# Moving weight preparation and accumulator copies by a tick in a fused Fourier / two-layer MLP kernel

## The chip, the cores and the metric

The kernel runs on one core of a Trainium2 chip. The metric is the device time of one launch in microseconds. Three runs of the kernel before gave 958.94, 959.30 and 959.51 us (median 959.3 us).

## What is computed

The input `x` has the shape (2, 3008, 256). The real part of its two-dimensional Fourier transform over the last two axes goes, as 6016 rows of 256 numbers, through two feed-forward layers of hidden width 2048, in float32:

```python
X = np.fft.fft(x, axis=1); X = np.fft.fft(X, axis=2); x = X.real.reshape(6016, 256)
h = x @ w_in
g = np.where(h > 0.0, h, np.exp(np.minimum(h, 0.0)) - 1.0)
x = g @ w_out
h = x @ w2_in
g = np.maximum(h, 0.0) + alpha * np.minimum(h, 0.0)
out = g @ w2_out
```

## The kernel before

**Numbers and blocks.** Products run on TensorE in a shortened float type. To keep float32 accuracy an operand is split into a rounded part, hi (written by ScalarE), and the rest, lo (written by GpSimd or VectorE), and a product is made in three passes: hi by hi, lo of the weight by hi, hi of the weight by lo (`PASSES`, line 465). The 6016 rows are cut into six blocks, each of two tiles (t = 0 and 1) of up to 512 columns. The last part of the transform, over the 256 columns, is folded into the first layer's `w_in`: `w_fold(c)` (lines 376 to 406) multiplies chunk c, a quarter of the hidden width, by a constant matrix with full float32 products (line 381) and splits the result.

**Ticks.** Layer one is 96 ticks, written out by the host loop in lines 900 and 901. One tick handles 128 hidden units f of one block. `SEGS` (line 42) sets the order: block 0 with f 0 to 7 in ticks 0 to 7, block 1 with f 0 to 7 in ticks 8 to 15, block 0 with f 8 to 15 in ticks 16 to 23, block 1 with the same in ticks 24 to 31, and then four blocks of 16 ticks. Tick t does, in this order on each engine's queue:

- the "pre" hooks of the tick;
- `gemm1(t)` on TensorE, six products (line 477), then on VectorE the correction `pt` (line 610) and the two halves `ht` (line 614), which read the product's two PSUM banks;
- on ScalarE hi of tick t-2 (line 589), then the "mid" hooks;
- if tick t-3 was the last of a segment (t = 10, 18, 26, 34, 50, 66, 82), `gemm2(t-3)` now, and the copy of the accumulators' t = 0 half by VectorE (`evac`, line 626);
- on ScalarE the relu (line 630) and the exponential (line 636 through tick 41; from tick 42 line 641, which writes two PSUM banks);
- on GpSimd lo of tick t-2 (line 595), on VectorE the combination of tick t-1 (line 582 or 579);
- in those seven ticks, the copy of the accumulators' t = 1 half (line 647). Where a segment starts at f = 0 (t = 10, 18, 50, 66, 82) ScalarE makes these copies, two of them (line 511);
- the "end" hooks, and in all other ticks `gemm2(t-3)`, twelve products (line 493).

For a segment's first f (but block 0's f = 0) and for its last, `gemm2` takes the three passes of each of the four accumulators one after the other; in the others the four lo passes come last. In both orders the second product of a `gemm2` reads lo of the weight.

**Weights.** A chunk of `w_out` is unpacked by ScalarE (`conv_y`, line 338) and by three VectorE steps (lines 356, 358 and 360), and then split in two halves (`w_split`, lines 412 to 423): each half has one ScalarE copy for hi (line 435) and one GpSimd subtraction for lo (line 436). `CONV1` (lines 53 to 58) lists, for a chunk, the tick of `conv_y` (a "mid" hook), the ticks of the three steps and the ticks of the two halves of the split (all of them "end" hooks, lines 776 to 783). Chunk 2 is read from f = 8 on, first by the `gemm2` in tick 19, and chunk 3 from f = 12 on, first by the `gemm2` in tick 23. `FOLD` (line 64) places `w_fold` of chunks 2 and 3, `STAGE_A1` (line 60) the first transform step of the second batch: `stage_a(1, c, i)` (lines 181 to 193) is two full float32 products (line 187) and two ScalarE copies (line 189). `KEEP` (lines 71 to 78) loads and unpacks second-layer chunks during layer one (load in the first tick given, `conv_y` and first step in the second tick, steps two and three in every second tick after). `PREP_0` (line 81) prepares the second layer's first operands; `b11` is one ScalarE copy ("mid") and one GpSimd subtraction ("end").

PSUM has eight banks: four accumulators, two "mm" and two "ee". Before tick 42 `gemm1`, `stage_a` and `w_fold` take the mm pair and the ee pair in turn; from tick 42 `gemm1` has the mm pair alone and the exponential the ee pair.

The second layer (pairs, lines 705 to 766) starts after tick 95, at about 463 us.

Of the kernel before, what the change touches and what calls it, by code (L numbers as in the profile page):

```python
# [43 lines left out]
E_PSUM = 42  # L44
# [8 lines left out]
CONV1 = [  # L53
    (('i', 1, 2), 8, (8, 9, 11), ()),
    (('i', 1, 3), 11, (12, 13, 14), ()),
    (('o', 1, 2), 14, (14, 15, 16), (17, 18)),
    (('o', 1, 3), 18, (18, 20, 21), (21, 22)),
]

STAGE_A1 = [  # L60
    (0, (7, 'pre'), (8, 'pre')), (1, (9, 'pre'), (11, 'pre')), (2, (12, 'pre'), (14, 'pre')), (3, (16, 'pre'), (17, 'pre')),
]
LOAD_X = {3: 9}
FOLD = {2: (13, 'pre', 0), 3: (15, 'mid', 0)}
LOAD_V = {(0, 2): 12, (1, 0): 24, (1, 1): 24, (1, 2): 24}
STAGE_B = {(0, 1): 5, (0, 2): 22, (1, 2): 32, (1, 0): 36, (1, 1): 40}
LOAD_ZB = {1: 6, 2: 29, 3: 45, 4: 61, 5: 77}
# [2 lines left out]

KEEP = [
    (("i", 2, 0), 31, 34, 81),
    (("o", 2, 0), 36, 39, 84),
    (("i", 2, 1), 45, 48, 88),
    (("o", 2, 1), 52, 55, 92),
    (("i", 2, 2), 59, 61, 95),
# [1 line left out]
]  # L78
FINAL_1 = [(84, "i", 0, 0), (86, "i", 0, 1), (88, "o", 0, 0), (90, "o", 0, 1), (92, "i", 1, 0), (94, "i", 1, 1)]
DIRECT = {("o", 2, 2): 95, ("o", 2, 3): 0}  # L80
PREP_0 = [("x", 62), ("t3", 64, 65), ("t1", 67, 68), ("b11", None, 69), ("t2", 74, 75), ("b21", None, 76), ("t4", 78, 82),
          ("b22", None, 83)]
FIRST = [
# [21 lines left out]
def tile_fft_moe_elu_moe_prelu(  # L105
# [361 lines left out]
    def gemm1(bl, f, two):  # L467
        n = BLOCKS[bl][2]
        c, o = divmod(f, 4)
        fs = slice(o * 128, (o + 1) * 128)  # L470
        w = wi[1, c]
        ps2 = []
        for t in range(2):
            p = mmtile(two)
            ops = [(w[:, a, t, fs], zt[bl][:, b, t, 0:n]) for a, b in PASSES]
            for i, (lhsT, rhs) in enumerate(ops):
                mm(out=p[:, 0:n], lhsT=lhsT, rhs=rhs, start=(i == 0), stop=(i == len(ops) - 1))  # L477
            ps2.append(p[:, 0:n])
        return ps2
# [16 lines left out]
    def evac(L, bl, f, first, last, ts, ds=(0, 1)):  # L496
        n = BLOCKS[bl][2]
        ac = accs[L, bl]
        if L == 1 and bl not in xs:
            xs[bl] = big.tile([128, 2, 2, 512], F32, tag="big", name="xs")  # L500
        for t in ts:
            for d in ds:
                if L == 1:
                    o = xs[bl][:, d, t, 0:n]
                else:
                    ot = wk.tile([128, 512], F32, tag="s", name="ot", bufs=4)
                    o = ot[:, 0:n]
                if first > 0:
                    tt(out=o, in0=ac[d][t][:, 0:n], in1=xs[bl][:, d, t, 0:n], op=ALU.add)
                elif t == 1:  # L510
                    act(out=o, in_=ac[d][t][:, 0:n], func=ACTF.Copy)  # L511
                else:
                    nc.vector.tensor_copy(out=o, in_=ac[d][t][:, 0:n])
                if L == 2:
                    for g, a, c0, m in pieces(bl):
                        nc.sync.dma_start(out=out[d * 128:(d + 1) * 128, c0 + t * BLK_N[g]:c0 + t * BLK_N[g] + m],
                                          in_=o[:, a:a + m])
            if L == 1 and last == NFT - 1 and 1 in ds:
                nc.sync.dma_start(out=xd[bl][:, :, t, 0:n], in_=xs[bl][:, :, t, 0:n])

    def pieces(bl):

        b, g, n = BLOCKS[bl]
        at_ = lambda b_, g_: 2 * (b_ * HALF + sum(BLK_N[:g_]))
        if bl != LONG:
            return [(g, 0, at_(b, g), n)]
        b0, g0, n0 = BLOCKS[SHORT]
        return [(g, 0, at_(b, g), n - MOVED), (g0, n - MOVED, at_(b0, g0) + n0, MOVED)]
# [39 lines left out]
    ticks = [(1, bl, f, f0, f1 - 1) for bl, f0, f1 in SEGS for f in range(f0, f1)]  # L568
    NT = len(ticks)
    LAG = 3  # L570

    def parts(t):
        return (slice(0, 1), slice(1, 2)) if t == 0 else (slice(0, 2),)

    def combine(t, some=None):
        s = st[t]
        if "x" in s:
            for i in range(2):
                stt(out=s["e"][:, i, :], in0=s["x"][i], scalar=-1.0, in1=s["h"][:, i, :], op0=ALU.add, op1=ALU.max)  # L579
        else:  # L580
            for i in some or parts(t):
                stt(out=s["e"][:, i], in0=s["e"][:, i], scalar=-1.0, in1=s["h"][:, i], op0=ALU.add, op1=ALU.max)  # L582

    def split_hi(t):
        s = st[t]
        s["hi"] = wk.tile([128, 2, 512], F32R, tag="hi", name="hi")
        s["lo"] = wk.tile([128, 2, 512], F32R, tag="lo", name="lo")
        for i in parts(t):
            act(out=s["hi"][:, i, 0:s["n"]], in_=s["e"][:, i], func=ACTF.Copy)  # L589

    def split_lo(t):
        s = st[t]
        n = s["n"]
        for i in range(2):
            nc.gpsimd.tensor_tensor(  # L595
                out=s["lo"][:, i, 0:n], in0=s["e"][:, i, :], in1=s["hi"][:, i, 0:n].bitcast(F32), op=ALU.subtract)

    def tick(t, pre, mid, end):
        cur = ticks[t] if t < NT else None
        for fn in pre:  # L600
            fn()
        if cur:
            L, bl, f = cur[:3]
            n = BLOCKS[bl][2]
            p = gemm1(bl, f, t >= E_PSUM)
            ht = wk.tile([128, 2, 512], F32, tag="h", name="ht")
            et = wk.tile([128, 2, 512], F32, tag="e", name="et", bufs=3)
            st[t] = dict(n=n, f=f, h=ht[:, :, 0:n], e=et[:, :, 0:n])
            pt = wk.tile([128, 512], F32, tag="s", name="pt", bufs=4)
            stt(out=pt[:, 0:n], in0=zb[bl][:, 0:n], scalar=an_sb[:, f:f + 1], in1=p[0], op0=ALU.mult, op1=ALU.add)  # L610
            for i, op in enumerate((ALU.add, ALU.subtract)):
                if t == 1:
                    combine(0, parts(0)[i:i + 1])
                tt(out=ht[:, i, 0:n], in0=pt[:, 0:n], in1=p[1], op=op)  # L614
        if t == 1:
            split_hi(0)
            split_lo(0)
        if t - 2 in st and t > 3:
            split_hi(t - 2)
        for fn in mid:  # L620
            fn()
        over = t < NT and t - LAG in st and ticks[t - LAG][2] == ticks[t - LAG][4]
        if over:
            s = st.pop(t - LAG)
            gemm2(*ticks[t - LAG], s["hi"], s["lo"])
            evac(*ticks[t - LAG], (0,))
        if cur:
            s = st[t]
            for i in parts(t):
                act(out=s["e"][:, i], in_=s["h"][:, i], func=ACTF.Relu, scale=-1.0)  # L630
                if t == 2:
                    combine(1)
                    split_hi(1)
                    split_lo(1)
                if t < E_PSUM or t == NT - 1:
                    act(out=s["e"][:, i], in_=s["e"][:, i], func=ACTF.Exp, scale=-1.0)
            if E_PSUM <= t < NT - 1:
                s["x"] = []
                for i in range(2):
                    s["x"].append(ps.tile([128, 512], F32, tag="ee", name="eet", bufs=2)[:, 0:s["n"]])  # L640
                    act(out=s["x"][i], in_=s["e"][:, i, :], func=ACTF.Exp, scale=-1.0)  # L641
        if t - 2 in st and t > 3:
            split_lo(t - 2)
        if t - 1 in st and t > 2:
            combine(t - 1)
        if over:
            evac(*ticks[t - LAG], (1,))
        for fn in end:
            fn()
        u = {2: 0, 3: None}.get(t, t - LAG)  # L650
        if u in st and t < NT:
            last_1(u)

    def last_1(u):
        s = st.pop(u)
        gemm2(*ticks[u], s["hi"], s["lo"])
# [113 lines left out]
    def at(t, fn, *a, where="pre"):  # L770
        hooks[where].setdefault(t, []).append(lambda: fn(*a))

    def at2(p, fn, *a, where="pre"):
        hooks[where].setdefault(1000 + p, []).append(lambda: fn(*a))
# [16 lines left out]
    with tc.manual_schedule():  # L791
# [45 lines left out]
        at(9, load, ("o", 1, 2))  # L837
        for c, (t, where, n) in FOLD.items():
            at(t, w_fold, c, where=where)
# [48 lines left out]
        for bl in range(2, NBLK):  # L888
            for i, (pre, mid) in enumerate(AHEAD):
                for where, todo in (("pre", pre), ("mid", mid)):  # L890
                    for what, *args in todo:
                        at2(bl * NFT // 2 - len(AHEAD) + i, does[what], bl, *args, where=where)
        for name, t, *cs in PREP_0:
            if name == "x":
# [5 lines left out]
        for t in range(NT):  # L900
            tick(t, *(hooks[w].get(t, []) for w in ("pre", "mid", "end")))
# [88 lines left out]
```

## Time and profile before

| | us |
|---|---|
| median of three runs | 959.3 |
| the profiled execution, its own time | 959.1 |
| its span from first to last instruction | 957.3 |
| TensorE busy | 945.2 |
| VectorE busy | 716.1 |
| ScalarE busy | 654.3 |
| GpSimd busy | 627.4 |

Times in the rows are microseconds from the start of the span. PE is TensorE's products, PEld its weight loads, DVE VectorE, ACT ScalarE, POOL GpSimd. A row of the timeline merges like instructions that follow each other: start, time from the first one's start to the last one's end, engine, line, operation, what is written and read, shapes and types, count, and in brackets the idle time of the engine just before and what ended it. The end of a product is modelled; successive products overlap, so their starts are what counts.

### The profile page before, as it was taken

The page shows a single profiled execution, that of the slowest core. Times are in us where ns is not written, and L with a number is a line of the kernel's source. Part 1 is how long each engine was busy: PE and PEld are TensorE (multiplying, and loading weights), DVE is VectorE, ACT ScalarE, POOL GpSimd, SP SyncE. Part 2 cuts the span into 40 slices and gives each one's busy share as a digit, 9 for nine tenths or more (in the row PEclk, how much of TensorE's full clock was granted, in tenths as well). Part 3 has the DMA queues.
Part 4 walks back from the last instruction along what each step waited for, and adds up shares of the span by engine and source line. Part 5 has one row for each costly group of instructions (what it writes and reads, how often), then busy time and mean ns, then how long its engine had stood idle before and what let it go on. Part 6 is the DMA issues. An engine that isn't in the chain of part 4 may idle for free.

```text
span 957.3 us, 12202 instructions
## 1 busy us (share of the span) xinstructions
PE 945.2 (99%) x4206; PEld 768.5 (80%) x4206; DVE 716.1 (75%) x1015; ACT 654.3 (68%) x915; POOL 627.4 (66%) x495
## 2 busy tenths in 40 slices
PE   9999999999999999999999999999999999999998
PEld 3677678799888877888888888889988888888886
DVE  2899899989999998887787675565666567566564
ACT  5778777767788887888765665656566566565553
POOL 1366578755968779987878855647565664664543
PEclk9999999999999999999999999999999999999999
DMA  8966222311322210130230110020020011001001
GB/s 326 321 187 161 58 78 88 100 49 41 100 84 98 90 45 34 45 110 22 69 130 1 39 45 0 7 83 1 1 73 10 0 45 45 1 1 45 0 1 45
DMA packets 27189, 64.10 MB, mean 67 GB/s; under 512 B 3124, under 2 KB 11572, under 8 KB 25080
## 3 DMA queue, kind: packets, MB, share of 16 engines
q1 hardware_dynamic: 25696, 62.09, 19.6%
q10 hardware_dynamic: 1176, 1.07, 0.3%
q8 instruction: 33, 0.54, 0.2%
q0 software_dynamic: 256, 0.17, 0.1%
q14 instruction: 28, 0.23, 0.1%
HBM read 41.53 MB, written 21.79 MB: 66 GB/s over the span
## 4 chain that ended last, share of the span: by engine, by line
PE 83%; DVE 10%; issue 2%; ACT 2%; POOL 1%; ACTq 0%; DVEq 0%; POOLq 0%
PE acc L493 45%; PE eet L672 13%; PE mmt L672 10%; PE mmt L477 7%; DVE ht L614 2%; DVE et L582 2%; PE eet L477 2%; DVE pt L610 2%; PE mmt L187 1%; DVE w L358 1%; POOL lo L595 1%; DVE et L579 1%; DVE w L360 1%; PE eet L381 1%; ACT et L630 1%
## 5 line engine op out<-in xcount | busy, mean ns | idle before, releaser
L493 PE MATMUL acc<-hi,wo 128*128 128x512 f32 (+1 forms) x1536 | 429.4, 386 | 2.8 <-ACT hi L589 1.5
L698 POOL TENSOR_TENSOR lo<-et,hi 128x512 fp32r<-128x512 f32 (+1 forms) x190 | 237.6, 1281 | 180.8 <-ACT hi L692 180.8
L595 POOL TENSOR_TENSOR lo<-et,hi 128x512 fp32r<-128x512 f32 (+1 forms) x192 | 276.3, 1461 | 94.4 <-ACT hi L589 48.9
L493 PEld LDWEIGHTS acc<-hi,wo 128*128 128x128 f32 x1536 | 287.9, 188 | 59.5 <-ACT xs L511 2.2
L493 PE MATMUL acc<-lo,wo 128*128 128x512 f32 (+1 forms) x768 | 258.4, 387 | 1.0 <-POOL lo L595 1.0
L692 ACT ACTIVATE hi<-et 128x1024 fp32r<-128x1024 f32 (+1 forms) x96 | 100.3, 1045 | 132.2 <-PE acc L493 69.9
L493 PEld LDWEIGHTS acc<-lo,wo 128*128 128x128 f32 x768 | 143.3, 188 | 30.9 <-POOL lo L595 3.9
L630 ACT ACTIVATE et<-ht 128x1024 f32<-128x1024 f32 (+2 forms) x97 | 100.3, 1034 | 64.0 <-DVE ht L614 62.2
L724 DVE TENSOR_TENSOR v<-mmt,p 128x512 f32<-128x512 f32 (+1 forms) x48 | 32.7, 680 | 143.0 <-ACT p L719 142.8
L477 PE MATMUL mmt<-zt,wi 128*128 128x512 f32 (+1 forms) x438 | 113.1, 391 | 0.8 <-DVE ht L614 0.4
L589 ACT ACTIVATE hi<-et 128x1024 fp32r<-128x1024 f32 (+2 forms) x97 | 99.4, 1024 | 5.5 <-DVE et L582 4.1
L614 DVE TENSOR_TENSOR ht<-pt,mmt 128x512 f32<-128x512 f32 (+1 forms) x148 | 93.8, 675 | 8.0 <-DVE pt L610 0.5
L477 PEld LDWEIGHTS mmt<-zt,wi 128*128 128x128 f32 x438 | 81.8, 188 | 19.9 <-issue 1.5
L749 ACT ACTIVATE et<-mmt 128x512 f32<-128x512 f32 (+1 forms) x96 | 55.8, 589 | 28.9 <-PE mmt L672 14.6
L582 DVE SCALAR_TENSOR_TENSOR et<-et,ht 128x1024 f32<-128x1024 f32 (+2 forms) x44 | 67.1, 1525 | 1.4 <-POOL lo L595 1.1
L610 DVE SCALAR_TENSOR_TENSOR pt<-zb,an_sb,mmt 128x512 f32<-128x512 f32 (+1 forms) x72 | 52.7, 731 | 20.0 <-PE mmt L477 19.9
L579 DVE SCALAR_TENSOR_TENSOR et<-eet,ht 128x512 f32<-128x512 f32 (+1 forms) x106 | 67.1, 675 | 0.0
L752 DVE SCALAR_TENSOR_TENSOR et<-et,oma_sb,eet 128x512 f32<-128x512 f32 (+1 forms) x96 | 66.1, 730 | 0.0
L752 DVE SCALAR_TENSOR_TENSOR et<-et,oma_sb,mmt 128x512 f32<-128x512 f32 (+1 forms) x96 | 66.0, 729 | 0.0
L641 ACT ACTIVATE eet<-et 128x512 f32<-128x512 f32 (+1 forms) x106 | 58.9, 588 | 3.7 <-DVE et L579 2.1
L672 PE MATMUL eet<-xo,wi 128*128 128x512 f32 (+1 forms) x216 | 59.8, 385 | 0.0
L672 PE MATMUL mmt<-xo,wi 128*128 128x512 f32 (+1 forms) x216 | 59.8, 385 | 0.0
(123 smaller groups left out, 1249.9 us busy)
## 6 DMA issues: line engine op xcount, KB each, us to landing
w<-w_in SPq DMA_DIRECT2D x8, 1024.0 KB, 9.7
w<-w_out SPq DMA_DIRECT2D x7, 1024.0 KB, 7.7
ud<-uc SPq DMA_DIRECT2D x20, 256.0 KB, 4.2
vt<-ud SPq DMA_DIRECT2D x5, 1024.0 KB, 5.0
xd<-xs SPq DMA_DIRECT2D x10, 512.0 KB, 3.4
xs<-xd SPq DMA_DIRECT2D x5, 1024.0 KB, 4.9
out_t<-ot SPq DMA_DIRECT2D x16, 256.0 KB, 2.2
xc<-x SPq DMA_DIRECT2D x5, 768.0 KB, 11.4
```

Source lines behind the costliest of these rows:

```text
L477: mm(out=p[:, 0:n], lhsT=lhsT, rhs=rhs, start=(i == 0), stop=(i == len(ops) - 1))
L493: mm(out=accs[L, bl][d][t][:, 0:n], lhsT=w[:, a, o, d * 128:(d + 1) * 128], rhs=(hi, lo)[b][:, t, 0:n], start=(f == first and i == 0), sto ...
L579: stt(out=s["e"][:, i, :], in0=s["x"][i], scalar=-1.0, in1=s["h"][:, i, :], op0=ALU.add, op1=ALU.max)
L582: stt(out=s["e"][:, i], in0=s["e"][:, i], scalar=-1.0, in1=s["h"][:, i], op0=ALU.add, op1=ALU.max)
L589: act(out=s["hi"][:, i, 0:s["n"]], in_=s["e"][:, i], func=ACTF.Copy)
L595: nc.gpsimd.tensor_tensor(out=s["lo"][:, i, 0:n], in0=s["e"][:, i, :], in1=s["hi"][:, i, 0:n].bitcast(F32), op=ALU.subtract)
L614: tt(out=ht[:, i, 0:n], in0=pt[:, 0:n], in1=p[1], op=op)
L630: act(out=s["e"][:, i], in_=s["h"][:, i], func=ACTF.Relu, scale=-1.0)
L672: mm(out=bank[:, 0:n], lhsT=w[:, a], rhs=x2[b][:, 0:n], start=(first and m == 0), stop=(last and m == 2), skip_group_check=True)
L692: act(out=s["hi"][f][:, :, 0:n], in_=s["g"][f], func=ACTF.Copy)
L698: eng.tensor_tensor(out=s["lo"][f][:, t, 0:n], in0=s["g"][f][:, t], in1=s["hi"][f][:, t, 0:n].bitcast(F32), op=ALU.subtract)
L752: stt(out=o, in0=o, scalar=oma_sb[:, 2 * j + f:2 * j + f + 1], in1=h, op0=ALU.mult, op1=ALU.add)
```

## The change

Layer-one `w_out` chunk 2 is unpacked and split one tick later, and so is chunk 3 except for its last two VectorE steps. The first half of `stage_a(1, 3)` goes from tick 16 to tick 15, and `w_fold(3)` from the "mid" place of tick 15 to the "pre" place of tick 16. The second-layer chunk ("o", 2, 0) is loaded and unpacked two ticks earlier. The split of `b11` goes from tick 69 to tick 70. In ticks 50, 66 and 82 ScalarE copies the t = 1 accumulators between the relu and the two exponentials, in place of after them.

```diff
 CONV1 = [
     (('i', 1, 2), 8, (8, 9, 11), ()),
     (('i', 1, 3), 11, (12, 13, 14), ()),
-    (('o', 1, 2), 14, (14, 15, 16), (17, 18)),
-    (('o', 1, 3), 18, (18, 20, 21), (21, 22)),
+    (('o', 1, 2), 15, (15, 16, 17), (18, 19)),
+    (('o', 1, 3), 19, (19, 20, 21), (22, 23)),
 ]
 STAGE_A1 = [
-    (0, (7, 'pre'), (8, 'pre')), (1, (9, 'pre'), (11, 'pre')), (2, (12, 'pre'), (14, 'pre')), (3, (16, 'pre'), (17, 'pre')),
+    (0, (7, 'pre'), (8, 'pre')), (1, (9, 'pre'), (11, 'pre')), (2, (12, 'pre'), (14, 'pre')), (3, (15, 'pre'), (17, 'pre')),
 ]
-FOLD = {2: (13, 'pre', 0), 3: (15, 'mid', 0)}
+FOLD = {2: (13, 'pre', 0), 3: (16, 'pre', 0)}
 KEEP = [
-    (("o", 2, 0), 36, 39, 84),
+    (("o", 2, 0), 34, 37, 84),
-PREP_0 = [("x", 62), ("t3", 64, 65), ("t1", 67, 68), ("b11", None, 69), ("t2", 74, 75), ("b21", None, 76), ("t4", 78, 82),
+PREP_0 = [("x", 62), ("t3", 64, 65), ("t1", 67, 68), ("b11", None, 70), ("t2", 74, 75), ("b21", None, 76), ("t4", 78, 82),
...
             if E_PSUM <= t < NT - 1:
+                if over:
+                    evac(*ticks[t - LAG], (1,))
                 s["x"] = []
                 for i in range(2):
...
-        if over:
+        if over and not E_PSUM <= t < NT - 1:
             evac(*ticks[t - LAG], (1,))
```

## Rows read from the trace of the kernel before

**Rows 1.** The page, busy time of each engine, share of the span, instructions.
```profile
PE 945.2 (99%) x4206; PEld 768.5 (80%) x4206; DVE 716.1 (75%) x1015; ACT 654.3 (68%) x915; POOL 627.4 (66%) x495
```

**Rows 2.** Waits of PE: who it waited for, us in total, times, longest.
```profile
PE eet L381 <- DVE w L360: 1.3, 2, 0.9
PE acc L493 <- ACT xs L511: 1.2, 1, 1.2
```

**Rows 3.** Timeline of ticks 14 and 15, PE and DVE.
```profile
108.48 1.52 PE L477 MATMUL mmt<-zt,wi 128*128 128x512 f32 x6
...
108.56 2.32 DVE L360 SCALAR_TENSOR_TENSOR w<-w,w 128x1024 int32<-128x1024 int32 x1
...
110.93 3.70 PE L381 MATMUL eet<-w,c_sb 128*128 128x512 f32 x8 [0.94 <-DVE w L360]
```

**Rows 4.** Timeline of ACT from the end of tick 17 to the end of tick 18.
```profile
129.96 0.61 ACT L435 ACTIVATE wo<-w 128x512 fp32r<-128x512 f32 x1
...
131.54 1.12 ACT L338 ACTIVATE w<-w 128x1024 f32<-128x1024 f32 x1
132.57 1.05 ACT L630 ACTIVATE et<-ht 128x1024 f32<-128x1024 f32 x1
...
134.61 1.07 ACT L511 ACTIVATE xs<-acc 128x512 f32<-128x512 f32 x2
135.56 0.63 ACT L435 ACTIVATE wo<-w 128x512 fp32r<-128x512 f32 x1
```

**Rows 5.** Timeline of PE in ticks 19 and 20.
```profile
134.31 0.62 PE L493 MATMUL acc<-hi,wo 128*128 128x512 f32 x2
...
137.03 1.52 PE L477 MATMUL mmt<-zt,wi 128*128 128x512 f32 x6
...
140.20 0.61 PE L493 MATMUL acc<-lo,wo 128*128 128x512 f32 x2
141.11 0.73 PE L493 MATMUL acc<-lo,wo 128*128 128x512 f32 x2 [0.29 <-POOL lo L595]
```

**Rows 6.** Timeline of DVE in ticks 17 and 18.
```profile
127.73 1.28 DVE L582 SCALAR_TENSOR_TENSOR et<-et,ht 128x1024 f32<-128x1024 f32 x1
129.75 0.75 DVE L610 SCALAR_TENSOR_TENSOR pt<-zb,an_sb,mmt 128x512 f32<-128x512 f32 x1 [0.74 <-PE mmt L477]
130.60 1.28 DVE L614 TENSOR_TENSOR ht<-pt,mmt 128x512 f32<-128x512 f32 x2
```

**Rows 7.** Timeline of POOL in ticks 17 to 19.
```profile
127.88 2.29 POOL L595 TENSOR_TENSOR lo<-et,hi 128x512 fp32r<-128x512 f32 x1
...
136.27 1.30 POOL L436 TENSOR_TENSOR wo<-w,wo 128x512 fp32r<-128x512 f32 x1 [0.81 <-ACT wo L435]
137.52 3.54 POOL L595 TENSOR_TENSOR lo<-et,hi 128x512 fp32r<-128x512 f32 x2
```

**Rows 8.** Timeline of ticks 21 to 23, POOL, ACT and PE.
```profile
150.61 0.63 ACT L435 ACTIVATE wo<-w 128x512 fp32r<-128x512 f32 x1 [0.34 <-DVE w L360]
...
155.11 0.62 ACT L435 ACTIVATE wo<-w 128x512 fp32r<-128x512 f32 x1
...
155.34 1.98 PE L493 MATMUL acc<-hi,wo 128*128 128x512 f32 x8
...
156.80 1.29 POOL L436 TENSOR_TENSOR wo<-w,wo 128x512 fp32r<-128x512 f32 x1
```

**Rows 9.** Timeline of PE in ticks 67 and 72.
```profile
345.47 0.73 PE L493 MATMUL acc<-hi,wo 128*128 128x512 f32 x2 [1.19 <-ACT xs L511]
...
367.70 0.73 PE L493 MATMUL acc<-lo,wo 128*128 128x512 f32 x2 [0.52 <-POOL lo L595]
```

**Rows 10.** Two stretches: length, busy PE, PEld, DVE, ACT, POOL, clock, DMA share, GB/s.
```profile
341.79:359.41 17.62, 16.39 (x71) 13.12 (x71) 17.20 (x27) 16.09 (x22) 13.53 (x12) 1.00 0.16 60
354.31:367.65 13.34, 12.87 (x57) 10.14 (x55) 12.35 (x19) 11.31 (x16) 13.18 (x12) 1.00 0.16 60
```

**Rows 11.** Timeline of ticks 37 and 41, ACT and DVE.
```profile
223.46 0.96 ACT L630 ACTIVATE et<-ht 128x904 f32<-128x904 f32 x1 [2.03 <-DVE ht L614]
...
241.91 2.19 DVE L358 SCALAR_TENSOR_TENSOR w<-w 128x1024 int32<-128x1024 int32 x1
```

## The prediction

> **What bounds the kernel.** I first read the page's busy times: TensorE is busy for 99% of the span [rows 1], so only its few waits can be saved, and any new wait is paid in full. Then I read TensorE's own waits by releaser [rows 2] and went to the timelines around each. Three waits lie where the change works: the fold of chunk 3 in tick 15 waits for VectorE's last unpacking step [rows 3], a `gemm2` in tick 20 waits for GpSimd [rows 5], and the `gemm2` of tick 67 waits for ScalarE's accumulator copies [rows 9]. Last I looked at who supplies the moved weights, and how long before their use: ScalarE in tick 18 [rows 4], GpSimd [rows 7], and the same one chunk later [rows 8]. One product is issued every 0.227 us: twelve from 134.31 to 137.03 [rows 5].
>
> **Fold and stage_a.** Before, the sixth product of `gemm1` starts at 108.48 + 5 x 0.227 = 109.61, the next could start at 109.84, and the fold starts at 110.93 [rows 3]: 1.1 us lost. Moved behind `stage_a`, `gemm1` and `gemm2` of tick 15, the fold starts several us after the unpacking step ends at 110.88. The same products are issued in another order, and the same copies go with them. The fold's ScalarE copies now stand ahead of hi(14), which is wanted only a tick later; its table of corrections goes out by a GpSimd DMA that is first needed four ticks later. So -1.1 us up to tick 18. Whether some of it is lost to a bank that VectorE frees late does not matter to the end, as the next step shows.
>
> **Chunk 2, tick 19.** This decides. `gemm2` in tick 19 is the first reader of chunk 2. Before, the first half's split stands at the end of tick 17, at 129.96 on ScalarE [rows 4], over 4 us ahead of its use at 134.31 [rows 5]. Now it stands at the end of tick 18, behind the relu, the exponential and the two accumulator copies of that tick. That is the place that the second half has before: hi at 135.56 [rows 4], lo on GpSimd at 136.27 [rows 7]. What goes earlier there: the unpacking (1.12 us) no longer delays the relu, but the relu still needs `ht`, which ends at 130.60 + 1.28 = 131.88 [rows 6], so it starts at 131.95 and not at 132.57: 0.6 us. VectorE's `ht` itself follows TensorE's 1.1 us, but an unpacking step (1.2 to 2.2 us) now sits at the end of tick 17, where VectorE idled 0.74 us [rows 6]: it comes between 1.1 us earlier and 0.5 us later; I take 0.6 us earlier, nearer to the short step, since GpSimd should be done by then. So hi starts at 135.56 - 1.2 = 134.35 and is there at 134.95, lo (1.30 us and 0.1 us to start) at 136.35, between 135.85 and 137.45. TensorE, due at 133.2, waits 1.75 us for hi, issues one product, and waits about 1.2 us for lo; eleven more products end at 138.85 instead of 137.03. The 1.1 us are gone and 1.8 us are lost on top (1.3 to 2.9). Queued behind this wait on TensorE is everything: `gemm1` of tick 20 and all that follows.
>
> **Tick 20.** There the wait for lo costs 141.11 - (140.20 + 2 x 0.227) = 0.45 us [rows 5]; its cause is the split at 136.27 ahead of lo(17) at 137.52 [rows 7]. In the new order lo(17) follows the first half's split, from 136.35 on, and takes two times 1.30 to 3.54 us [rows 7], to 139.9 (141.0 from the late end), while TensorE wants it at 138.85 + 14 x 0.227 = 142.0. So -0.45 us, and +1.35 us in all so far (0.85 to 2.45).
>
> **Chunk 3, tick 23.** The same once more. The first half's split goes from 150.61 to the place of the second half: hi at 155.11, lo at 156.80 to 158.09; the first reader starts at 155.34 [rows 8]. Its second product, due at 155.57, needs lo. With 0.63 us less of ScalarE work ahead (the split that was at 150.61), lo is there at 157.5: +1.9 us, between 1.3 and 2.5 (nothing gained on ScalarE). All engines take their work from `gemm1` of the same tick, so the earlier wait does not let them run ahead.
>
> **The copies in tick 66.** The wait of 1.19 us for the first copy [rows 9] goes: the copies no longer stand behind two exponentials. But the gain does not last. VectorE works without a pause from 341.79 to 359.41, 17.20 of 17.62 us [rows 10], so what it feeds does not come earlier; GpSimd works from 354.31 to 367.65 without a pause (13.18 of 13.34 us), and at 367.70 TensorE waits for just that [rows 9]. TensorE arrives there earlier and waits longer. I count 0, with -1.2 as the other end. The split of `b11` moves within that unbroken GpSimd stretch, still ahead of the lo that ends it: 0, hidden by the same wait. In ticks 50 and 82 TensorE does not wait for the copies (there is one such wait in all [rows 2], the one of tick 67); the exponentials come about 1.1 us later, the length of two copies [rows 4], and are read a tick after: 0.
>
> **The chunk ("o", 2, 0).** Its load moves past the accumulator stores on SyncE's queue, to a buffer free since tick 32, so it starts earlier. Its ScalarE unpacking falls into an idle stretch of 2.03 us in tick 37 [rows 11]. Its third VectorE step now stands in tick 41 where the second did (2.19 us [rows 11]): no change. If that cover were gone, the unpacking's 1.12 us [rows 4] at most.
>
> **Sum**, against the profiled execution's 959.1 us: -1.1 + 2.9 (tick 19) - 0.45 + 1.9 + 0 = +3.25, so 962.35; against the median of 959.3, 962.5. Its own bounds: 0.85 + 1.3 = +2.15 to 2.45 + 2.5 = +4.95, 961.4 to 964.3.
>
> [...] GpSimd's lo took 2.29 us at 127.88, having started 0.15 us after VectorE's combination (127.73 to 129.01), against 1.30 us alone [rows 6, 7]. [...]
>
> **Rivals.** (a) *Faster: the splits are in time.* If hi and lo of the new places were ready by 133.2 and 155.6, only the gains stand: -1.1 - 0.45, and up to -1.2 in tick 66, 956.6 to 957.7. It decides at whether ScalarE reaches the split 1.7 us sooner than I work out. For it: the waits of before show how little slack it takes. Against it: relu, exponential and copies, 3 us in a row, stand ahead of it on an in-order queue, and the relu cannot start before `ht`. (b) *The gain in tick 66 stays*, if GpSimd's stretch shortens by its contended steps falling elsewhere: 962.5 - 1.2 = 961.3. (c) *The splits meet VectorE's combination* and take 2.29 us in place of 1.30 both times: 964.5. (d) *The moved fold does not save its wait*, because TensorE waits for its banks in tick 17 instead: the end stays as forecast, since tick 19 is set by ScalarE and GpSimd.
>
> **Chances.** Forecast (with d) 0.54, (a) 0.14, (b) 0.17, (c) 0.13, else 0.02. A measurement tells 0.2%, 1.9 us, from no change: faster means under 957.4, slower over 961.2. Of (a) a small part stays within 0.2%, of (b) nearly half. Faster 0.13, same 0.15, slower 0.72. The range 960.0 to 965.0 holds the forecast, (b) and most of (c), and leaves (a) out.
>
> **What would show it.** In the changed trace: no wait before line 381 in tick 16; in tick 19 TensorE waiting for ScalarE's line 435 and GpSimd's line 436, and again in tick 23; the wait for line 511 in tick 67 gone, and the wait for GpSimd in tick 72 longer by as much. Wrong would be: lines 435 and 436 finished before the `gemm2` of ticks 19 and 23 reaches them, or the arrival in tick 72 earlier than before by what tick 67 saved.

## The result: 7 us slower, twice what was forecast

The changed kernel takes 966.2 us (median of 6 executions, 965.5 to 967.6) against 959.2 us (958.9 to 959.6) for the kernel before on the same chip: a ratio of 1.0075, 95% interval 1.0062 to 1.0088. The forecast was 962.5 us in 960.0 to 965.0. The direction was right, the size half of the truth, and the time lies outside the range.

The profiled execution took 967.46 us, with a span of 965.7 us against 957.3 before. The page of the changed kernel, its busy times and its row of granted clocks (the share of its full clock that TensorE was given, in tenths) in 40 slices:

```profile
PE 949.3 (98%) x4206; PEld 770.8 (80%) x4206; DVE 716.6 (74%) x1015; ACT 654.4 (68%) x915; POOL 622.5 (64%) x495
...
PEclk9999989999999999999999999999999999999999
```

Beside [rows 1], TensorE runs the same 4206 products, but is busy 4.1 us longer, although not one instruction was added; and the sixth slice (121 to 145 us) shows a lower clock. So a part of the 8.4 us is waiting and a part is products that took longer. TensorE's waits, by whom it waited for (us in total, times, longest), beside [rows 2]:

```profile
PE acc L493 <- ACT wo L435: 2.9, 2, 2.6
PE acc L493 <- POOL wo L436: 1.7, 2, 0.9
...
PE mmt L477 <- DVE pt L610: 0.7, 1, 0.7
```

The first two rows are new: the splits of chunks 2 and 3, 4.6 us in four waits. New too is the wait for VectorE's `pt`. The wait of 0.9 us before line 381 in tick 15 and the one of 1.2 us for the copies in tick 67 are gone. Timeline of TensorE in ticks 15, 16, 18, 19, 20, 23 and 72 (columns as in the rows ahead of the prediction):

```profile
109.88 1.95 PE L477 MATMUL eet<-zt,wi 128*128 128x512 f32 x6
...
114.39 3.59 PE L381 MATMUL mmt<-w,c_sb 128*128 128x512 f32 x8
...
131.82 1.52 PE L477 MATMUL eet<-zt,wi 128*128 128x512 f32 x6
135.97 0.50 PE L493 MATMUL acc<-hi,wo 128*128 128x512 f32 x1 [2.63 <-ACT wo L435]
137.33 0.79 PE L493 MATMUL acc<-hi,wo 128*128 128x512 f32 x1 [0.86 <-POOL wo L436]
...
138.34 1.05 PE L493 MATMUL acc<-hi,wo 128*128 128x512 f32 x2
...
142.19 2.17 PE L477 MATMUL mmt<-zt,wi 128*128 128x512 f32 x6
144.20 1.99 PE L493 MATMUL acc<-hi,wo 128*128 128x512 f32 x8
...
161.01 0.50 PE L493 MATMUL acc<-hi,wo 128*128 128x512 f32 x1 [0.24 <-ACT wo L435]
162.36 1.88 PE L493 MATMUL acc<-hi,wo 128*128 128x512 f32 x7 [0.85 <-POOL wo L436]
...
374.93 0.73 PE L493 MATMUL acc<-lo,wo 128*128 128x512 f32 x2 [0.46 <-POOL lo L595]
...
376.16 0.73 PE L493 MATMUL acc<-lo,wo 128*128 128x512 f32 x2 [0.50 <-POOL lo L595]
```

The fold runs in tick 16 without a wait. In tick 19 the two forecast waits stand where they were expected, hi and then lo with one product between. What was not expected comes behind them: two products take 0.86 us (138.34 to 139.20 in the full trace) where two took 0.45 us before, down to the `gemm1` of tick 20. Three stretches of the same execution, with length, busy PE, PEld, DVE, ACT, POOL, granted clock, DMA share and GB/s:

```profile
128.00:133.00 5.00, 5.00 (x24) 4.10 (x22) 4.90 (x6) 2.71 (x4) 3.59 (x3) 1.00 0.65 196
133.40:137.30 3.90, 0.50 (x1) 0.19 (x1) 3.80 (x5) 3.90 (x6) 1.31 (x2) 0.93 0.16 67
137.30:143.20 5.90, 5.87 (x14) 4.62 (x15) 2.76 (x2) 4.18 (x5) 5.14 (x4) 0.50 0.00 0
```

While it waits, TensorE does one product in 3.9 us. Then, for 5.9 us, the granted clock is 0.50: 14 products take the time of 26 at the 0.227 us of before. **So the stall is paid twice**, in waiting and in slow work after it.

Where the 8.4 us arise, read from the starts of the same products in both profiled executions:

| place | lead or lag of the changed kernel after it, us | this step, us |
|---|---|---|
| fold, up to tick 18 | -1.13 | -1.13 |
| tick 19, wait for hi | +1.66 | +2.79 |
| tick 19, wait for lo | +2.79 | +1.13 |
| tick 19 and 20 at 0.50 clock | +5.81 | +3.02 |
| tick 20, wait for lo gone | +5.25 | -0.56 |
| ticks 21 to 23 | +6.93 | +1.68 |
| ticks 24 to 30, small waits for GpSimd shorter | +6.72 | -0.21 |
| ticks 41 to 43, above all the wait for `pt` | +7.82 | +1.10 |
| ticks 44 to 67, a new wait of 0.33 us for VectorE's `ht` at 350.06 | +8.15 | +0.33 |
| tick 67, wait for copies gone | +6.66 | -1.49 |
| ticks 68 and 69, waits for VectorE | +7.86 | +1.20 |
| tick 72, waits for GpSimd | +8.46 | +0.60 |

The profiled execution is one of the two longest (967.5 us, mean granted clock 0.996); the other four have 965.5 to 966.4 us at 0.998. By estimate, 5.9 us at 0.50 in a span of 965.7 us alone take the mean to 0.997, so in those four the half-speed stretch was shorter. Steps are therefore also priced by medians below.

### The profile page after: what moved, and what is told of

The parts are those of the page before. It is cut to its first block, busy times and chain, and to the rows that moved or that the text cites. A ratio compares the mean times of both kernels' runs of the same rounds, so it can differ in the third digit from the quotient of the medians.

```text
span 965.7 us, 12198 instructions
## 1 busy us (share of the span) xinstructions
PE 949.3 (98%) x4206; PEld 770.8 (80%) x4206; DVE 716.6 (74%) x1015; ACT 654.4 (68%) x915; POOL 622.5 (64%) x495
## 4 chain that ended last, share of the span: by engine, by line
PE 83%; DVE 9%; ACT 3%; issue 2%; DMA 1%; POOL 1%; ACTq 0%; DVEq 0%; POOLq 0%
PE acc L493 46%; PE eet L674 13%; PE mmt L674 10%; PE mmt L477 7%; DVE ht L614 2%; PE eet L477 2%; DVE et L582 2%; DVE pt L610 1%; PE mmt L187 1%; DVE w L358 1%; DVE w L360 1%; PE mmt L381 1%; DMA nd<-dt 1%; ACT et L630 1%; DVE et L579 1%
```

## Experiments

Each kernel is the one before or the changed one with one or a few parts exchanged; all are compared with the kernel before on the same chip. Its medians there, 959.15 to 959.22 us, are close enough to set the experiments beside each other.

**1. The change with chunk 2 as before.**

```diff
-    (('o', 1, 2), 15, (15, 16, 17), (18, 19)),
+    (('o', 1, 2), 14, (14, 15, 16), (17, 18)),
```

> The changed kernel with the line of w_out chunk 2 as before (unpacking from tick 14, splits in ticks 17 and 18). Theory: the wait in tick 19 (2.8 us for hi, 1.1 us for lo) and the slow products behind it (about 3 us in the profiled execution) are all chunk 2's. They go, the fold's 1.1 us stay saved, the wait of 0.56 us in tick 20 comes back: about 961.3 us, no product at 0.43 us pitch near 137 us. Rival: the wait only moves to another supplier in ticks 18 to 20, or the clock falls for another reason: 964 us or more.

Measured: 961.18 us (961.01 to 962.32, 11 executions), 1.0022 [1.0013, 1.0031]. Timeline of TensorE, ticks 19, 20 and 23:

```profile
133.40 0.61 PE L493 MATMUL acc<-hi,wo 128*128 128x512 f32 x2
...
140.09 0.73 PE L493 MATMUL acc<-lo,wo 128*128 128x512 f32 x2 [0.18 <-POOL lo L595]
...
154.79 0.50 PE L493 MATMUL acc<-hi,wo 128*128 128x512 f32 x1 [0.30 <-ACT wo L435]
156.16 1.88 PE L493 MATMUL acc<-hi,wo 128*128 128x512 f32 x7 [0.86 <-POOL wo L436]
```

With one line undone, 5.0 of the 7.0 us are gone: no wait in tick 19, no slow product behind it, and the small wait for lo in tick 20 is back. Tick 23 is as in the changed kernel, and there 0.30 and 0.86 us of waiting are followed by seven products in 1.88 us; in the changed kernel, behind 0.24 and 0.85 us there, the granted clock is 1.00 from 160.5 to 164.5.

**2. Chunks 2 and 3 as before.** The same edit and

```diff
-    (('o', 1, 3), 19, (19, 20, 21), (22, 23)),
+    (('o', 1, 3), 18, (18, 20, 21), (21, 22)),
```

> The changed kernel with both chunks' lines as before. Theory: the wait of 1.6 us in tick 23 goes as well, 1.7 us below the kernel with chunk 2 alone put back, about 959.6 us; what is left above the fold's gain is a new wait in tick 43 (0.9 us) and ticks 67 to 72 (0.6 us). Rival: the loss of tick 23 was only carried over from tick 19 and is gone already with chunk 2: no difference to that kernel.

Measured: 960.10 us (959.82 to 961.50), 1.0011 [1.0002, 1.0020]. The wait of tick 23 is gone too, which is worth 961.18 - 960.10 = 1.1 us, less than the 1.7 us expected: in tick 24 this kernel loses 0.32 us that experiment 1 does not. What is left of the change should by the forecast be 1.1 us faster than before, and is 0.95 us slower. So something besides the splits costs 2 us.

**3. The wait of tick 19 filled with work.** Twelve products into a free bank ahead of the `gemm2` of tick 19; nothing reads their result, and nothing is left out.

```diff
+FILL = 12
...
+    def filler(n):
+        p = ps.tile([128, 512], F32, tag="mm", name="mmt", bufs=2)
+        for i in range(n):
+            mm(out=p, lhsT=wi[1, 0][:, 0, 0, 0:128], rhs=zt[0][:, 0, 0, :], start=True, stop=True)
...
     def last_1(u):
+        if u == 16:
+            filler(FILL)
...
```

> The changed kernel with 12 products more (2.7 us of TensorE, result unused) ahead of the gemm2 of tick 19, where TensorE waits. Theory: the wait is filled, no product after it runs at half speed, and the kernel with more work is faster: about 963 us, all runs within 0.5 us. Rival 1: the half speed has nothing to do with the wait: 966 us, as the changed kernel, with slow products near 137 us. Rival 2: the products come on top: 968 us or more.

Measured: 964.79 us (964.43 to 965.20, 5 executions), 1.0057 [1.0045, 1.0070]. Timeline of TensorE (line 660 is the filler):

```profile
133.74 2.88 PE L660 MATMUL mmt<-zt,wi 128*128 128x512 f32 x12
136.53 0.50 PE L494 MATMUL acc<-hi,wo 128*128 128x512 f32 x1
137.89 0.51 PE L494 MATMUL acc<-hi,wo 128*128 128x512 f32 x1 [0.86 <-POOL wo L437]
...
140.50 1.52 PE L478 MATMUL mmt<-zt,wi 128*128 128x512 f32 x6
141.86 1.98 PE L494 MATMUL acc<-hi,wo 128*128 128x512 f32 x8
```

and one stretch of it, with the granted clock third from the end:

```profile
138.00:144.00 6.00, 6.00 (x27) 4.98 (x28) 4.76 (x6) 3.94 (x6) 6.00 (x4) 1.00 0.00 1
```

More work, less time, though 1.8 us above what was expected. The wait for lo is the same 0.86 us, but the clock behind it is 1.00, and from the second product of `gemm2` in tick 19 to the first one in tick 20 it takes 141.86 - 137.89 = 3.97 us, against 144.20 - 137.33 = 6.87 us in the changed kernel. The difference of 2.9 us is the price of the half-speed clock in the profiled execution of the changed kernel; by medians it is 966.19 - 964.79 = 1.4 us, since most executions of the changed kernel are shorter than the profiled one. The rival, that the products were slow because their weights or GpSimd's work slowed them, falls: both are there as before.

**4. The filler with six products.** The same edit with `FILL = 6`.

> The changed kernel with 6 products (1.4 us) in place of 12 ahead of the gemm2 of tick 19, so that half of the wait for hi stays. If TensorE is at full speed after it, the gemm2 ends when hi and lo allow it, as with 12: 964.8 us. If waits of 1.4 and 1.1 us with one product between still bring the half speed, 966 us.

Measured: 964.64 us (964.53 to 966.16, 5 executions), 1.0059 [1.0047, 1.0072]. The profiled execution is the long one. Timeline of TensorE, then one stretch with the granted clock third from the end:

```profile
133.34 1.52 PE L660 MATMUL mmt<-zt,wi 128*128 128x512 f32 x6
136.12 0.49 PE L494 MATMUL acc<-hi,wo 128*128 128x512 f32 x1 [1.26 <-ACT wo L436]
137.48 0.80 PE L494 MATMUL acc<-hi,wo 128*128 128x512 f32 x1 [0.86 <-POOL wo L437]
...
140.63 0.39 PE L494 MATMUL acc<-lo,wo 128*128 128x512 f32 x1
```

```profile
137.40:140.70 3.30, 3.22 (x8) 2.55 (x9) 2.81 (x2) 3.16 (x4) 3.30 (x3) 0.51 0.00 0
```

Here waits of 1.26 and 0.86 us were followed by a granted clock of 0.51 for 3.3 us. Seven products from 137.48 to 140.63 lose 3.15 - 7 x 0.227 = 1.6 us. The other four executions were 1.2 to 1.6 us shorter; they have no profile. Two of them have a mean granted clock of 1.00, so they kept the full clock here. The other two have 0.998, like the profiled one; that they kept it too is inferred from their times only.

**5. The first halves' splits ahead of the relu, in the same ticks.**

```diff
-        at(t, w_split, kind, layer, c, i, where="end")
+        at(t, w_split, kind, layer, c, i, where="end" if i else "mid")
```

> The changed kernel with the first half's split of both chunks in the same ticks (18 and 22) but ahead of the relu in place of at the tick's end. Theory: it is the place behind relu, exponential and copies that makes hi and lo late, not the tick; ahead of the relu, hi stands about 4 us earlier on ScalarE and lo ahead of GpSimd's two tick subtractions, so the waits in ticks 19 and 23 go with the slow products: 959.5 to 960.5 us, like both lines put back. Rival: one tick ahead is too late in any place, 963 us or more.

Measured: 961.87 us (961.24 to 963.78, 9 executions), 1.0026 [1.0016, 1.0036], 4.3 us less than the changed kernel but slower than expected. Timeline of TensorE, ticks 19, 21 and 23:

```profile
134.87 0.73 PE L493 MATMUL acc<-hi,wo 128*128 128x512 f32 x2 [0.25 <-ACT xs L511]
...
146.31 0.72 PE L493 MATMUL acc<-lo,wo 128*128 128x512 f32 x2 [0.87 <-POOL lo L595]
...
155.89 1.98 PE L493 MATMUL acc<-hi,wo 128*128 128x512 f32 x8
```

Nothing waits for a split any more, in either tick. So of the 6.1 us between the changed kernel and experiment 2, 4.3 us came from the place behind relu, exponential and copies. The other 1.8 us stay with the later tick. ScalarE in ticks 17 and 18, and GpSimd from tick 19 on:

```profile
130.07 0.63 ACT L435 ACTIVATE wo<-w 128x512 fp32r<-128x512 f32 x1 [0.19 <-DVE w L360]
132.18 1.06 ACT L630 ACTIVATE et<-ht 128x1024 f32<-128x1024 f32 x1 [1.47 <-DVE ht L614]
...
140.43 1.28 POOL L436 TENSOR_TENSOR wo<-w,wo 128x512 fp32r<-128x512 f32 x1
141.67 4.58 POOL L595 TENSOR_TENSOR lo<-et,hi 128x512 fp32r<-128x512 f32 x2
```

The split is not in the relu's way: behind it ScalarE is idle for 1.47 us until `ht` is there, which on VectorE comes behind the unpacking step at the end of tick 17, as in the changed kernel (2.32 us at 127.82 there). So the copies come late, and TensorE waits for them in tick 19. In tick 21 it waits 0.87 us for lo of tick 18, which stands on GpSimd behind the second half's split, still at the end of tick 19, and ends at 146.25; in experiment 2 it ended at 143.66.

**6. The fold alone** (before, with only the lines of `STAGE_A1` and `FOLD` changed).

> The kernel before with the move of the fold and of the first half of stage_a(1, 3) alone. Theory: the 1.1 us wait in tick 15 goes and no later wait takes it back, 958.1 us. Rival: the waits for GpSimd in tick 20 (0.45 us) or for VectorE in tick 43 grow by what was saved: 959.2 us.

Measured: 958.31 us (957.90 to 958.92), 0.9990 [0.9982, 0.9999]: 0.84 us gained. The profiled execution is 1.06 us ahead at tick 16 and 0.95 us at tick 90.

**7. The chunk ("o", 2, 0) alone.**

```diff
-    (("o", 2, 0), 36, 39, 84),
+    (("o", 2, 0), 34, 37, 84),
```

> The kernel before with the second-layer chunk (o, 2, 0) two ticks earlier, alone. Theory: the wait of 0.86 us before the gemm1 of tick 43 that the changed kernel has is this edit's, since its second VectorE step (1.2 us) stands at the end of tick 39 in place of the first (0.7 us), in the ticks where VectorE also has stage_b's subtractions: 960.0 us, with PE waiting for DVE at tick 43. Rival: that wait belongs to another edit, 959.2 us.

Measured: 960.51 us (960.04 to 960.95) against 959.21, 1.0012 [1.0003, 1.0021]: 1.3 us lost by an edit that was costed at nothing. Timeline of VectorE, GpSimd and TensorE, ticks 39 to 43:

```profile
233.90 1.21 DVE L358 SCALAR_TENSOR_TENSOR w<-w 128x1024 int32<-128x1024 int32 x1
...
238.09 1.93 DVE L582 SCALAR_TENSOR_TENSOR et<-et,ht 128x904 f32<-128x904 f32 x1
...
236.76 2.30 POOL L595 TENSOR_TENSOR lo<-et,hi 128x452 fp32r<-128x452 f32 x2 [3.74 <-issue]
...
246.08 0.88 PE L477 MATMUL mmt<-zt,wi 128*128 128x452 f32 x3 [0.70 <-DVE pt L610]
```

and the same steps of the kernel before, which are not among the rows ahead of the prediction:

```profile
233.64 0.68 DVE L356 TENSOR_SCALAR w<-w 128x1024 int32<-128x1024 int32 x1
...
237.58 1.09 DVE L582 SCALAR_TENSOR_TENSOR et<-et,ht 128x904 f32<-128x904 f32 x1
...
236.50 3.21 POOL L595 TENSOR_TENSOR lo<-et,hi 128x452 fp32r<-128x452 f32 x2 [3.74 <-issue]
```

The third step does stand in tick 41 where the second stood. But the second now stands at the end of tick 39 where the first stood: 1.21 us in place of 0.68. (Everything there runs 0.26 us later from the start-up on.) An idle stretch of 0.2 us on VectorE takes up a part, and the combination comes 0.51 us later, 0.25 us of it from the edit. That turns round which engine goes first. Before, the combination came ahead of GpSimd's second lo, and the two lo took 3.21 us. Now they take 2.30 us and end at 239.06, and the combination, which starts at 238.09 ahead of that end, takes 1.93 in place of 1.09 us and ends at 240.02. VectorE has no pause up to tick 43, so its `pt` and then its `ht` are late there; the second wait, 0.39 us, is like one of 0.36 us before. By the starts of the products, ticks 41 to 43 cost 1.09 us here and 1.10 us in the changed kernel. The changed kernel has the same two waits, 0.69 us at 252.56 and 0.39 us at 253.82.

**8. The copies alone** (before, with only the edit of ticks 50, 66 and 82).

> The kernel before with the accumulator copies between relu and exponentials alone. Theory: TensorE gains 1.3 us or more in tick 67 and gives it back by tick 72, to VectorE's banks and to GpSimd's unbroken stretch: 959.2 us, no difference. Rival: the gain stays, 957.9 us, and what eats it in the changed kernel is the move of b11.

Measured: 959.55 us (959.14 to 959.87), 1.0003 [0.9994, 1.0012]. Timeline of TensorE, ticks 67 to 72:

```profile
351.57 0.98 PE L477 MATMUL mmt<-zt,wi 128*128 128x512 f32 x3 [0.43 <-DVE ht L614]
...
363.29 0.73 PE L493 MATMUL acc<-lo,wo 128*128 128x512 f32 x2 [0.28 <-POOL lo L595]
...
368.17 0.73 PE L493 MATMUL acc<-lo,wo 128*128 128x512 f32 x2 [0.49 <-POOL lo L595]
```

The wait for the copies is gone, and is paid back, for the most part to VectorE: by the starts of the products the lead behind tick 67, 1.24 us over the kernel before, is spent in tick 69. GpSimd takes 0.54 us more in tick 71 (the wait of 0.28 us). The wait of 0.49 us in tick 72 is not a payment: the kernel before has it too, 0.52 us [rows 9].

**9. The split of `b11` alone**, at 70 in place of 69.

> The kernel before with the split of b11 in tick 70 alone. Theory: it stays within GpSimd's unbroken stretch that ends with the lo of tick 72, so the wait there stays as it is: 959.2 us. Rival: the 0.6 us that the changed kernel loses between ticks 67 and 72 are its own: 959.8 us.

Measured: 959.18 us (958.78 to 959.49), 1.0000 [0.9991, 1.0009], with the waits of ticks 67 and 72 as before.

**10. Fold, copies, and `b11` out of the busy stretch** (at 85 in place of 69), to see whether the copies' gain lasts once GpSimd has less to do.

> The kernel before with the moves of the fold and of stage_a, the copies between relu and exponentials, and the split of b11 in tick 85, where GpSimd has room. Theory: with 1.3 us less on GpSimd ahead of the lo of tick 72, the wait there (0.8 us) goes and the gain of tick 67 (1.3 us) stays: 958.3 - 1.5 to 2.1, 956.2 to 956.8 us. Rival: VectorE's unbroken stretch alone holds TensorE back, 958.3 us.

Measured: 957.52 us (957.16 to 957.77), 0.9982 [0.9973, 0.9991], slower than expected. GpSimd's wait in tick 72 is gone, but VectorE's stays, a line of TensorE's timeline:

```profile
350.46 0.96 PE L477 MATMUL mmt<-zt,wi 128*128 128x512 f32 x3 [0.42 <-DVE ht L614]
```

**11. The same without the copies.**

> The kernel before with the moves of the fold and of stage_a and the split of b11 in tick 85, without the move of the copies. Theory: in tick 72 the wait for GpSimd goes (0.8 us), the one of 1.3 us in tick 67 stays: 957.5 us, no slower than with the copies moved too, whose gain VectorE takes back. Rival: the copies' part of the 0.8 us that the other kernel gained is most of it: 958.3 us.

Measured: 957.38 us (957.14 to 958.36), 0.9982 [0.9973, 0.9991]. TensorE waits 1.20 us for the copies in tick 67 and for nobody from there to tick 72:

```profile
344.67 0.72 PE L493 MATMUL acc<-hi,wo 128*128 128x512 f32 x2 [1.20 <-ACT xs L511]
```

With and without the copies the end is the same within their spreads. TensorE waits either ahead of this stretch, for ScalarE, or in it, for VectorE; both profiled executions start the `gemm2` of tick 73 at 367.94. This and the kernel of experiment 10 beat both kernels, the changed one by 8.7 to 8.8 us, the one before by 1.7 to 1.8 us. How much of it is `b11` alone at 85 was not tried; beside the fold alone it is 958.31 - 957.38 = 0.9 us.

## Why the prediction was right in direction and wrong in size

The parts measured alone add up: fold -0.84, the chunk ("o", 2, 0) +1.3, copies +0.34, `b11` 0, together +0.8 us, against +0.95 us for experiment 2, which has these four.

- **Fold, forecast -1.1.** Right: -1.13 us in the profile, -0.84 us by medians.
- **Chunk 2, tick 19, forecast +2.9.** Right in mechanism: ScalarE's hi behind relu, exponential and copies, then GpSimd's lo. The lo was right (1.2 forecast, 1.13 measured). The hi was mis-sized: 1.75 us forecast, 2.79 measured. The step that failed is "it comes between 1.1 us earlier and 0.5 us later; I take 0.6 us earlier, nearer to the short step, since GpSimd should be done by then". VectorE's and GpSimd's steps in the changed kernel, tick 17, and what hung on them on ScalarE:

```profile
127.82 2.32 DVE L360 SCALAR_TENSOR_TENSOR w<-w,w 128x1024 int32<-128x1024 int32 x1
...
130.89 1.29 DVE L614 TENSOR_TENSOR ht<-pt,mmt 128x512 f32<-128x512 f32 x2
...
125.52 3.52 POOL L595 TENSOR_TENSOR lo<-et,hi 128x512 fp32r<-128x512 f32 x2 [2.56 <-issue]
...
132.28 1.06 ACT L630 ACTIVATE et<-ht 128x1024 f32<-128x1024 f32 x1 [2.29 <-DVE ht L614]
...
135.28 0.63 ACT L435 ACTIVATE wo<-w 128x512 fp32r<-128x512 f32 x1
```

  GpSimd was not done: its two lo end at 129.04, in the middle of the unpacking step, which took 2.32 us; such a step took 1.21 us at 149.36 in the kernel before, with GpSimd idle. The prediction's own rows said so: lo at 127.88 takes 2.29 us [rows 7], which 1.1 us earlier ends at 129.07, while the step can start where the combination ends, 129.01 - 1.1 = 127.9 [rows 6]. So `ht` starts at 130.89, 0.29 us later than before [rows 6] and not 0.6 us earlier, and hi starts at 135.28 where 134.35 was forecast: 0.93 us of the error. It came near the late bound that the prediction itself gave.
- **The missing term.** The sum knew waits only. That TensorE's granted clock would be 0.50 for 5.9 us behind the waits of tick 19 was in no case and no rival: the sum put it at nothing, without a reason. It cost 2.9 us in the profiled execution and 1.4 us by medians (experiment 3). This and the chunk ("o", 2, 0), below, are why the time lies outside the range: without them it would be 966.2 - 1.4 - 1.3 = 963.5 us.
- **Tick 20, forecast -0.45.** Right: -0.56 us. **Chunk 3, tick 23, forecast +1.9.** Right in mechanism, a bit high: 1.68 us in the profile over ticks 21 to 23, 1.1 us by medians (experiments 1 and 2), since small waits for GpSimd behind it, in ticks 24 to 30, get shorter.
- **The chunk ("o", 2, 0), forecast 0.** Wrong: +1.10 us in the profile, +1.3 us by medians (experiment 7). The step that failed is "Its third VectorE step now stands in tick 41 where the second did (2.19 us): no change". It looked at the tick where a step of like length stood, not at the tick where the step before it had become longer.
- **Copies and `b11`, forecast 0.** Near in number, +0.34 us by medians for the copies (an interval that holds 0) and 0 for `b11`; half right in mechanism. The gain of 1.49 us in tick 67 is taken back by tick 72, but not as the prediction said it would show, by a wait for GpSimd in tick 72 "longer by as much": 1.20 us go to VectorE in ticks 68 and 69, and the waits in tick 72 are 0.96 us in place of 0.52. With GpSimd relieved (experiment 10) VectorE still took its part. That the number came out near 0 is in part luck.

Of the rivals, (a) falls, since the first half's split was late for both chunks; (b) falls, since the gain of tick 67 was gone by tick 72; (c), a slower lo, did not happen (the lo of the first halves, at 135.99 and 161.03, took 1.28 us each), but its neighbour did, on VectorE's side: the unpacking step in tick 17 took 2.32 us beside GpSimd's lo; (d) did not happen, no bank was late in tick 17.

## What to carry to other kernels

When the engine that bounds a kernel is given a new stall of a few us, count the stall and then look at the granted clock behind it: here it was 0.50 for 5.9 us behind waits of 2.63 and 0.86 us. When a step moves one tick later, ask what it queues behind *within* that tick; here the same tick ahead of the relu was 4.3 us cheaper than behind it. And a moved chain of steps has to be compared tick by tick on each engine, since a step that is 0.5 us longer in one place can turn round which of two engines goes first: in experiment 7 the combination then took 1.93 us in place of 1.09.

## What the runs showed of the hardware

- **TensorE's granted clock behind a wait.** Waits of 2.63 and 0.86 us with one product between were followed by a granted clock of 0.50 for 5.9 us; waits of 1.26 and 0.86 us by 0.51 for 3.3 us in the profiled one of five executions (experiment 4); waits of 0.24 and 0.85 us (tick 23 of the changed kernel) by 1.00 from 160.5 to 164.5, and one of 0.86 us alone (experiment 3) by 1.00 from 138 to 144. At which wait this changes was not measured. The six executions of the changed kernel took 965.5 to 967.6 us, but only one of them has a trace.
- **Some VectorE steps took longer beside GpSimd's lo.** VectorE's unpacking step that began at 127.82 in the changed kernel took 2.32 us and ended 1.10 us after GpSimd's lo (129.04 to 130.14); in the kernel before, the same line at 149.36 took 1.21 us while GpSimd was idle (148.36 to 151.32, below). The combination of experiment 7 took 1.93 us and ended 0.96 us after the lo (239.06 to 240.02), while such a combination that came ahead of the second lo took 1.09 us (237.58 in the kernel before). There a shift of 0.25 us became a loss of 0.84 us (1.93 - 1.09). `ht`, whose operands come partly from PSUM, did not take longer: in the changed kernel its two halves took 1.29 us at 130.89, beside two lo of GpSimd (130.11 to 132.66) that took 1.29 us each, and 1.29 us at 88.20 with GpSimd idle (85.44 to 90.36). What sets the steps apart was not shown. The unpacking step of the kernel before, and the next step of GpSimd:

```profile
149.36 1.21 DVE L360 SCALAR_TENSOR_TENSOR w<-w,w 128x1024 int32<-128x1024 int32 x1
...
151.32 1.30 POOL L436 TENSOR_TENSOR wo<-w,wo 128x512 fp32r<-128x512 f32 x1 [2.96 <-ACT wo L435]
```
